# RWKV-5 attention and a SoLU feed-forward block on one core: the decay load on another queue, and a new order for the last chunk

## The chip, the cores and the metric

The kernel runs on one core of a Trainium2 chip. The metric is the device time of one execution in microseconds; lower is better. Besides the plain times there is one profiled execution, with a trace of every instruction and every DMA.

## What is computed

The first half is RWKV-5 attention: for each of 4 batches and 8 heads, a 48 x 48 state is carried over 768 steps and decayed by a vector `w`, with a bonus `u` for the step's own key. The second half is a feed-forward block over the 3072 rows of 384 values that result.

```python
cur = einsum('bhd,bhe->bhde', u * kt, vt)
y[:, :, t] = einsum('bhd,bhde->bhe', rt, state + cur)
state = w[..., None] * state + einsum('bhd,bhe->bhde', kt, vt)
...
h = x @ w_in                               # 384 -> 1024
e = exp(h - max(h)); solu = h * e / sum(e)
ln = (solu - mean) / sqrt(var + 1e-6) * g_ln
out = ln @ w_out                           # 1024 -> 384
```

## The kernel before, in words

The rows are cut into N = 24 chunks of 128 (6 time steps by 4 batches). For each chunk the kernel loads k, r and v, weights them with tables of powers of the decay, forms scores and outputs on TensorE, and then runs the chunk through the feed-forward block. One long function, `direct_path`, writes out the order of all instructions by hand (`manual_schedule`). Every engine works through its own list in exactly the order in which the calls stand, so moving a call moves each instruction that it issues within that engine's list, and each DMA within the list of its queue. Almost every DMA is issued by SyncE (SP). Two small ones are not: `w` by GpSimd (line 493) and `u` by ScalarE (line 496).

**The start.** `w` lands in `wq` (4 x 2 x 48 values). GpSimd issues that DMA as its first instruction of the kernel's own work, then makes the identity matrix `ident`. TensorE runs a few idle multiplications on `ident` (`spin(3)`), turns `wq` into a column (`wd_ps`, line 636), and spreads `u` over the partitions (`u_ps`, line 638). VectorE first clears pads and the score banks (lines 494 to 504). Then it builds the power tables `tab` from `wd_ps` by doubling (lines 643 to 656). From `tab` come the first keys and queries (`turn_r(0)` at 778, `turn_k(0)` at 786), GpSimd's `wide` (line 1313), `weigh(0)` (lines 734 and 735), and everything after them. The first loads of k, r, v and of the weights are all issued ahead of time by SP (lines 594 to 608).

**The feed-forward of a chunk.** `exponential` is on ScalarE. `unit_a` (VectorE, lines 1049 and 1053) makes `solu` and its sum. `unit_b` (ScalarE, line 1061) makes the sum of squares. `deviation` makes from these the factor and shift of the normalisation in four operations on [128 x 1] columns, all on GpSimd: variance (1073), the power -1/2 (1075), the scale (1079) and the shift (1081). `normalise` applies them (ScalarE, 1093). `halve_ln` splits the 32-bit words into 16-bit halves (1118) and starts a DMA transpose on SP (1107). `join_ln` puts the turned halves together again (VectorE, 1112).

**The way out.** Chunks leave in pairs (18 and 19, 20 and 21, 22 and 23 are the last three). `row_sums_12` and `row_sums_34` (VectorE, 1192 to 1198) make sums of halves `s[1]` to `s[4]` of a pair. Seven blocks of 4 matrix multiplications each (line 1202; the trace shows 8 instructions a block) then give both chunks:

- `both_a(l, (0,))` and `(1,)` need only the first chunk of the pair. `(2,)` needs `s[2]`, and so both chunks, and also the copy at 1219 of the bank that it adds to.
- `take_a` adds and copies the banks out (1228, 1230).
- `both_b` has blocks for `s[1]` (its bank is copied out at 1235), `s[3]` and `s[4]`. With `check_sums` a tiny product `n_ps` (706) is put between the last two blocks.
- `both_c` (block for `sums_w[4]`, additions 1249 or 1262 and 1267, a DMA at 1268) and `both_d` (copy at 1278 or 1275, a DMA at 1279 or 1276) finish the pair.

**The checks.** The kernel tests that all weights lie in a range. `check_next` reads one loaded piece with ScalarE (582, `mag`) and has SP load the next piece (524). `check_least` reduces `mag` on VectorE (590). After the 14th piece, `compare_sums` (VectorE, 691 to 700) reduces all tests to one column `low`, which `n_ps` sums on TensorE. If the test fails, a slower general path runs afterwards. Here it doesn't.

The last calls, lines 1771 to 1820, are where the change lies. In them i = 23, j = 21, and l goes through 18, 20, 22.

Of the kernel before, what the change touches and what calls it, by code (L numbers as in the profile page):

```python
# [12 lines left out]
ALU = mybir.AluOpType  # L13
# [386 lines left out]
def direct_path(  # L400
# [29 lines left out]
    nc = tc.nc  # L430
    B, H, S, D = r.shape
# [5 lines left out]
    dff = moe_w_in.shape[1]  # L437
# [47 lines left out]
    wq = const.tile([HP, 2, P], F32, name="wq")  # L485
# [4 lines left out]
    w_out_sb = const.tile([128, KF, dm], F32, name="w_out_sb")  # L490
    decays = const.tile([128, HP], F32, name="decays")

    nc.gpsimd.dma_start(out=wq[:, :, 0:D], in_=w.rearrange("(a q) d -> a q d", q=2))
    nc.vector.memset(wq[:, :, D:], 1.0)
    u_row = u_bc[0:1].rearrange("p h d -> p (h d)")
    nc.scalar.dma_start(out=u_row, in_=u.rearrange("h d -> (h d)").unsqueeze(0))
# [82 lines left out]
    def check_words(j):  # L579
        raw = raws.pop(j)  # L580
        mag = wpool.tile([128, raw.shape[1]], F32, tag="mag", name="mag", bufs=1)
        nc.scalar.activation(out=mag, in_=raw[:, :, 1].bitcast(F32), func=ACT.Abs,
                             accum_out=total[:, j : j + 1])
        mags.append((j, mag))
# [3 lines left out]
    def check_least():  # L588
        for j, mag in mags:
            nc.vector.tensor_reduce(out=least[:, j : j + 1], in_=mag, axis=AX.X, op=ALU.min)  # L590
        mags.clear()
# [32 lines left out]
    neg_half = const.tile([128, 1], F32, name="neg_half")  # L624
# [15 lines left out]
    for vt in vts:  # L640
        nc.scalar.activation(out=vt[:, 1].rearrange("p h x -> p (h x)"),
                             in_=ident[:, 0:1].to_broadcast([128, H * P]), func=ACT.Copy, scale=0.0)
    nc.vector.tensor_scalar(out=pw[:, 0, 0], in0=wd_ps, scalar1=LOW, scalar2=HIGH,
                            op0=ALU.max, op1=ALU.min)
    nc.vector.tensor_copy(out=decays, in_=wd_ps)
    for j in range(8):
# [5 lines left out]
        else:  # L652
            n = 1 << (j - 1)
# [24 lines left out]
    N = len(units)  # L678
    stats = const.tile([128, 5, N], F32, name="stats")
# [388 lines left out]
        unit_a(i)  # L1068
        unit_b(i)

    def deviation(i, j):
        ss, var, rstd = (stats[:, n, i:j] for n in (2, 3, 4))
        nc.gpsimd.tensor_scalar(out=var, in0=ss, scalar1=1.0 / dff, scalar2=1e-6 * dff ** 2,  # L1073
                                op0=ALU.mult, op1=ALU.add)
        nc.gpsimd.tensor_tensor(out=rstd, in0=var, in1=neg_half.to_broadcast([128, j - i]), op=ALU.pow)
        i = max(i, SEVEN)
        if i < j:
            tot, shift, scale, rstd = (stats[:, n, i:j] for n in (1, 2, 3, 4))
            nc.gpsimd.tensor_scalar(out=scale, in0=rstd, scalar1=-float(dff), scalar2=1.0,
                                    op0=ALU.mult, op1=ALU.mult)  # L1080
            nc.gpsimd.tensor_tensor(out=shift, in0=tot, in1=rstd, op=ALU.mult)  # L1081

    def normalise_late(i):
        if SEVEN <= i < N:
# [4 lines left out]
    def normalise(i):  # L1089

        if SEVEN <= i < N:
            solu = live[i]["solu"]
            nc.scalar.activation(out=solu, in_=solu, func=ACT.Identity,  # L1093
                                 scale=stats[:, 3, i : i + 1], bias=stats[:, 2, i : i + 1])
# [16 lines left out]
    def join(words, turned):  # L1111
        nc.vector.tensor_copy(out=words.bitcast(U16).rearrange("p n (t o) -> p o n t", o=2),  # L1112
                              in_=turned)
# [7 lines left out]
    def join_ln(i):  # L1121
        X = live[i]
        if i not in ROOM:
            X["lnT"] = fpool.tile([128, KF, 128], F32, name="lnT")
        else:
            X["lnT"] = bigs[ROOM[i]].rearrange("p (f t) -> p f t", f=KF)
        join(X["lnT"], X["turned"])
# [67 lines left out]
    def row_sums_34(i, engine):  # L1195
        one, two, s = live[i]["lnT"], live[i + 1]["lnT"], live[i]["s"]
        engine.tensor_tensor(out=s[3], in0=one[:, 0:KH], in1=two[:, 0:KH], op=ALU.subtract)
        engine.tensor_tensor(out=s[4], in0=one[:, KH:KF], in1=s[2], op=ALU.subtract)

    def block(dst, rows, weights, start=False):  # L1200
        for f in range(KH):
            nc.tensor.matmul(dst, rows[:, f], weights[:, f], start=(start and f == 0),  # L1202
                             stop=(f == KH - 1), skip_group_check=True)
# [3 lines left out]
    def rows_out(i):  # L1207
        if i < N - 6:
            return fpool.tile([128, dm], F32, name="o")
        return apool.tile([128, H, P], F32, tag="kp", name="kp",  # L1210
                          bufs=5).rearrange("p h d -> p (h d)")[:, 0:dm]

    def both_a(i, which=(0, 1, 2)):
        X = live[i]
        if 0 in which:
            X["o"], X["o2"] = rows_out(i), rows_out(i + 1)
            X["a"], X["e"] = (psM.tile([128, NH], F32, tag="m", name="o_ps") for _ in range(2))
            block(X["a"], X["lnT"][:, 0:KH], upper[:, :, left], True)
            X.get("copy", nc.scalar.copy)(out=X["o"][:, left], in_=X["a"])
        if 1 in which:  # L1220
            block(X["e"], X["lnT"][:, KH:KF], lower[:, :, left], True)
        if 2 in which:
            block(X["a"], X["s"][2], sums_w[2])

    def take_a(i, engine):
        X = live[i]
        if engine == "DVE":
            nc.vector.tensor_tensor(out=X["o"][:, left], in0=X["e"], in1=X["o"][:, left], op=ALU.add)
        else:
            X.get("copy", nc.scalar.copy)(out=X["o"][:, right], in_=X["a"])  # L1230

    def both_b(i, between=None, later=False):
        X = live[i]
        block(X["e"], X["s"][1], sums_w[1], True)
        X.get("copy", nc.scalar.copy)(out=X["o2"][:, right], in_=X["e"])
        if not later:
            both_b2(i, between)

    def both_b2(i, between=None):
        X = live[i]  # L1240
        block(X["a"], X["s"][3], sums_w[3])
        if between:
            between()
        block(X["e"], X["s"][4], lower[:, :, right])

    def both_c_sum(i, also=False):
        X = live[i]
        o2 = X["o2"]
        nc.vector.tensor_tensor(out=o2[:, right], in0=X["a"], in1=o2[:, right], op=ALU.add)
        X["summed"] = True  # L1250
        if also:
            o = X["o"]
            nc.vector.tensor_tensor(out=o[:, right], in0=X["e"], in1=o[:, right], op=ALU.add)
            X["summed"] = 2

    def both_c(i):
        X, Y = live.pop(i), live.pop(i + 1)
        ending[i] = X
        o, o2, a, e = (X[n] for n in ("o", "o2", "a", "e"))
        rows, rows2 = (out[ds(b * S + c * T, T)] for b, c in (units[i], units[i + 1]))  # L1260
        if not X.get("summed"):
            nc.vector.tensor_tensor(out=o2[:, right], in0=a, in1=o2[:, right], op=ALU.add)
        block(a, Y["lnT"][:, KH:KF], sums_w[4])
        if i + 2 == N:
            nc.sync.dma_start(out=rows2[:, right], in_=o2[:, right])
        if X.get("summed") != 2:
            nc.vector.tensor_tensor(out=o[:, right], in0=e, in1=o[:, right], op=ALU.add)
        nc.sync.dma_start(out=rows, in_=o)

    def both_d(i):  # L1270
        X = ending.pop(i)
        (b, c), o2, a = units[i + 1], X["o2"], X["a"]
        rows2 = out[ds(b * S + c * T, T)]
        if i + 2 == N:
            nc.vector.tensor_copy(out=o2[:, left], in_=a)
            nc.sync.dma_start(out=rows2[:, left], in_=o2[:, left])
        else:
            nc.scalar.copy(out=o2[:, left], in_=a)
            nc.sync.dma_start(out=rows2, in_=o2)
# [31 lines left out]
    for q in range(2):  # L1311
        rows = slice(q * P, q * P + D)
        nc.gpsimd.tensor_tensor(out=wide.rearrange("p (a q) -> p a q", q=2)[P : P + D, :, q],
                                in0=back[rows, :, 0], in1=pw[rows, 0, 0], op=ALU.mult)
# [75 lines left out]
    for i in range(LA, LA + LO):  # L1390
        j = i - LA
# [51 lines left out]
    def check_next():  # L1443
        for p in checked:
            check_words(p)
        checked[:] = [checks.pop(0)] if checks else []
        for p in checked:
            load_weights(p, "check", 1)
# [8 lines left out]
    i = LA + LO  # L1457
    j, l = i - LA, 0
    load(i + 5, "kr")
    decay(i + 3)  # L1460
    diagonal(i + 1)
    deviation(0, j)
    ffn_in(j)
    halve_k(i + 3)
# [35 lines left out]
    for i in range(LA + LO + 2, ELEVEN, 2):  # L1500
        j, l = i - LA, i - LA - LO
# [41 lines left out]
        if l == EARLY + 4:  # L1543
            deviation(j, j + 1)
# [86 lines left out]
    for i in range(ELEVEN, N - 1, 2):  # L1631
        j, l = i - LA, i - LA - LO
# [82 lines left out]
    i = N - 1  # L1715
    j, l = i - LA, i - LA - LO
# [62 lines left out]
    both_b(l)  # L1779
    unit_a(i)  # L1780
    unit_b(i)
    deviation(i, N)
    halve_ln(j + 1)
    both_c_sum(l)
    both_c(l)
    join_ln(l + 2)
    join_ln(l + 3)
    row_sums_12(l + 2)
    row_sums_34(l + 2, nc.vector)
    both_d(l)  # L1790
    both_a(l + 2, (0,))
    normalise(i)
    halve_ln(i)
    check_next()

# [2 lines left out]
    both_a(l, (1, 2))  # L1798
    take_a(l, "DVE")
    take_a(l, "ACT")  # L1800
    join_ln(l + 2)
    both_b(l)
    check_least()
    both_c(l)
    both_d(l)
    check_next()
    join_ln(l + 3)
    row_sums_12(l + 2)
    check_least()

    l += 2
    both_a(l)
    take_a(l, "DVE")
    take_a(l, "ACT")
    check_least()
    compare_sums()
    row_sums_34(l, nc.vector)
    both_b(l, check_sums)
    both_c(l)
    both_d(l)  # L1820
# [43 lines left out]
```

## Time and profile before

| what | us |
|---|---|
| runs (median of 3; lowest, highest) | 325.33 (325.25, 325.44) |
| the profiled execution, its own time | 326.05 |
| its span, first to last instruction | 324.3 |
| TensorE busy | 308.9 (95%) |
| VectorE busy | 264.6 (82%) |
| GpSimd busy | 250.9 (77%) |
| ScalarE busy | 245.0 (76%) |
| granted TensorE clock | 0.998 |
| DMA traffic | 52.64 MB, mean 162 GB/s |

How to read it: a busy share is an average over the span, and TensorE's is near its limit. Whether a change of order helps is read in the stage that it touches, from the chain of work that ended last. This chain goes back from the last instruction: at each step it goes to whatever released that instruction, or to the one before it on its engine. By engine, it lies on TensorE for 58% of the span, on GpSimd for 17%, on VectorE for 12%, on waits for a DMA for 3% and on ScalarE for 2%. Timeline rows give start, length, engine, line and operation, and in brackets the idle time of the engine just before the row and what ended it.

### The profile page before, as it was taken

To read this page: it belongs to the slowest core of one execution; us is meant where nothing else is said; L and a number is where in the kernel's file an instruction comes from. 1 tells how busy PE (TensorE), PEld (TensorE's weight loads), DVE (VectorE), ACT (ScalarE), POOL (GpSimd) and SP (SyncE) were. 2 spreads that over 40 slices of the span, in tenths; PEclk is the share of its full clock that TensorE was granted. 3 is DMA by queue.
4 is the path that set the end of the run, shared out by engine and by line. 5 is a ranking of instruction groups with operands and counts; after the bars stand their busy time and mean duration, and the time that the engine had idled before them with its cause. 6 is when DMAs were issued, how large, how long until landed. Compare 5 with 4: busy or idle time off the path is not lost.

```text
span 324.3 us, 9699 instructions
## 1 busy us (share of the span) xinstructions
PE 308.9 (95%) x3903; PEld 216.7 (67%) x3903; DVE 264.6 (82%) x446; ACT 245.0 (76%) x418; POOL 250.9 (77%) x268
## 2 busy tenths in 40 slices
PE   5999999999999999999999999999999999999972
PEld 3875566555456457677678668668677676779972
DVE  6796999998887979999788699789979945868570
ACT  2875888888559788868968969949969978786410
POOL 4899878889999999999999999979978274275000
PEclk9999999999999999999999999999999999999999
DMA  8999999479999998996999999986757535674821
GB/s 165 255 255 200 207 244 169 75 140 139 194 169 173 174 183 144 159 193 106 167 186 164 176 195 225 197 171 133 143 152 161 92 103 147 144 172 102 166 91 61
DMA packets 165800, 52.64 MB, mean 162 GB/s; under 512 B 158321, under 2 KB 161522, under 8 KB 165746
## 3 DMA queue, kind: packets, MB, share of 16 engines
q1 hardware_dynamic: 165712, 51.92, 82.2%
q8 instruction: 33, 0.54, 0.7%
q14 instruction: 21, 0.17, 0.2%
q0 software_dynamic: 32, 0.00, 0.0%
q10 hardware_dynamic: 2, 0.00, 0.0%
HBM read 26.75 MB, written 4.72 MB: 97 GB/s over the span
## 4 chain that ended last, share of the span: by engine, by line
PE 58%; POOL 17%; DVE 12%; issue 5%; DMA 3%; ACT 2%; SPq 0%; POOLq 0%; ACTq 0%; DVEq 0%
PE o_ps L1202 22%; PE h_ps L969 16%; PE h_part L1003 9%; POOL rp L728 3%; POOL rku L734 3%; POOL big L754 3%; POOL kp L721 3%; PE y_ps L881 2%; PE at L819 2%; POOL rku L735 2%; DVE solu L1053 2%; DVE big L832 2%; DMA raw<-in_moe_w_out_dram 1%; PE y_ps L858 1%; PE h_part L881 1%
## 5 line engine op out<-in xcount | busy, mean ns | idle before, releaser
L969 PE MATMUL h_ps<-w_in_sb,xT 128*128 128x512 f32 x216 | 97.0, 598 | 0.0
L969 PEld LDWEIGHTS h_ps<-w_in_sb,xT 128*128 128x128 f32 x216 | 39.9, 190 | 45.1 <-issue 42.4
L1118 ACT COPY halves<-solu 128x2048 uint16<-128x2048 uint16 x23 | 43.6, 1897 | 1.2 <-DVE stats L1049 1.1
L1112 DVE COPY big<-halves 128x2048 uint16<-128x2048 uint16 x21 | 33.7, 1612 | 2.9 <-DMA halves<-halves 2.7
L721 POOL TENSOR_TENSOR kp<-kpad,kdec 128x512 f32<-128x512 f32 x24 | 34.1, 1423 | 0.7
L1112 DVE COPY lnT<-halves 128x2048 uint16<-128x2048 uint16 x18 | 30.1, 1684 | 1.5 <-DMA halves<-halves 1.4
L735 POOL TENSOR_TENSOR rku<-rku,rpad 128x384 f32<-128x384 f32 x24 | 29.0, 1210 | 1.9
L832 DVE COPY_PREDICATED big<-later_half,at 64x512 f32<-64x512 uint32 x40 | 29.4, 736 | 0.7
L734 POOL TENSOR_TENSOR rku<-kpad,u_bc 128x384 f32<-128x384 f32 x24 | 29.8, 1240 | 0.2
L754 POOL TENSOR_SCALAR_AFFINE_SELECT big<-own 64x512 f32<-64x512 f32 x40 | 27.7, 692 | 1.8
L1202 PE MATMUL o_ps<-w_out_sb,ma 128*128 128x192 f32 x160 | 28.1, 328 | 0.0
L1202 PEld LDWEIGHTS o_ps<-w_out_sb,ma 128*128 128x128 f32 x160 | 26.2, 190 | 1.9 <-issue 1.6
L728 POOL TENSOR_TENSOR rp<-rpad,rdec 128x512 f32<-128x512 f32 x15 | 25.5, 1703 | 0.0
L977 ACT ACTIVATE e<-h_ps 128x1024 f32<-128x1024 f32 x18 | 18.4, 1022 | 8.7 <-PE h_ps L969 8.6
L1073 POOL TENSOR_SCALAR stats<-stats 128x1 f32<-128x1 f32 (+2 forms) x14 | 7.2, 516 | 22.7 <-ACT e L1061 22.0
L1061 ACT ACTIVATE e<-solu,stats 128x1024 f32<-128x1024 f32 x20 | 23.0, 1148 | 2.1 <-DVE solu L1053 2.1
L1053 DVE SCALAR_TENSOR_TENSOR solu<-h_ps,stats,e 128x1024 f32<-128x1024 f32 x18 | 23.1, 1284 | 1.5
L1093 ACT ACTIVATE solu<-solu,stats 128x1024 f32<-128x1024 f32 x17 | 21.0, 1232 | 2.4 <-POOL stats L1081 2.4
L1157 PE MATMUL o_ps<-w_out_sb,lnT 128*128 128x384 f32 x64 | 21.6, 491 | 0.0
L1202 PE MATMUL o_ps<-w_out_sb,lnT 128*128 128x192 f32 x112 | 19.8, 330 | 0.0
L956 POOL TENSOR_TENSOR vt<-vt,wide 48x384 f32<-48x384 f32 x16 | 19.1, 1210 | 0.8
L1202 PEld LDWEIGHTS o_ps<-w_out_sb,lnT 128*128 128x128 f32 x112 | 18.3, 190 | 1.6 <-issue 1.4
(196 smaller groups left out, 703.6 us busy)
## 6 DMA issues: line engine op xcount, KB each, us to landing
raw<-in_moe_w_out_dram SPq DMA_DIRECT2D x16, 384.0 KB, 4.1
kpad<-in_k_dram SPq DMA_DIRECT2D x24, 192.0 KB, 5.0
rpad<-in_r_dram SPq DMA_DIRECT2D x24, 192.0 KB, 5.0
vt<-in_v_dram SPq DMA_DIRECT2D x40, 96.0 KB, 3.7
raw<-in_moe_w_in_dram SPq DMA_DIRECT2D x7, 512.0 KB, 6.3
out_dram<-o SPq DMA_DIRECT2D x18, 192.0 KB, 3.1
raw<-in_moe_w_in_dram SPq DMA_DIRECT2D x10, 256.0 KB, 3.4
out_dram<-kp SPq DMA_DIRECT2D x5, 192.0 KB, 3.0
```

The source lines that it names most:

```text
L721: nc.gpsimd.tensor_mul(X["kp"].rearrange("p h d -> p (h d)"), kpads[i % NLD].rearrange("p h d -> p (h d)"), kdec.rearrange("p a d -> p (a ...
L728: nc.gpsimd.tensor_mul(X["rp"].rearrange("p h d -> p (h d)"), rpads[i % NLD].rearrange("p h d -> p (h d)"), rdec.rearrange("p a d -> p (a ...
L734: engine.tensor_mul(rku, kpads[i % NLD][:, :, 0:D], u_bc)
L735: engine.tensor_mul(rku, rku, rpads[i % NLD][:, :, 0:D])
L754: nc.gpsimd.affine_select(out=G[rows, c].rearrange("p a q u -> p (a q) u"), in_=X["own"][rows].to_broadcast([U, H, U]), compare_op=ALU.is_ ...
L832: nc.vector.copy_predicated(X["G"][rows, c].rearrange("p a q u -> p q a u"), later_half[rows].unsqueeze(1).to_broadcast([U, 2, HP, U]), X[ ...
L969: nc.tensor.matmul(h_ps[:, ts(n, NX)], X["xT"][:, j, :], w_in_sb[:, j, ts(n, NX)], start=(j == 0), stop=(j == KD - 1))
L1003: nc.tensor.matmul(dst, rows, weights, start=start, stop=True, skip_group_check=True)
L1053: nc.vector.scalar_tensor_tensor(out=solu, in0=X["h"], scalar=rs, in1=X["e"], op0=ALU.mult, op1=ALU.mult, accum_out=tot)
L1112: nc.vector.tensor_copy(out=words.bitcast(U16).rearrange("p n (t o) -> p o n t", o=2), in_=turned)
L1118: copy(out=both.rearrange("p (o n) -> p o n", o=2), in_=split(X["solu"]))
L1202: nc.tensor.matmul(dst, rows[:, f], weights[:, f], start=(start and f == 0), stop=(f == KH - 1), skip_group_check=True)
```

## The change

Three things are changed.

1. The DMA of `w` is issued by ScalarE instead of GpSimd, ahead of that of `u`.
2. `deviation` is split into `variance`, `root` and `shifts`, which can be put on different engines. For the last chunk (23), `variance` and `shifts` go to VectorE, and only the power stays on GpSimd. They stand between the two joins of the pair 20, 21: the first join, then the variance, the power, `both_c`, the shifts, and the second join. `normalise(23)` now stands before `both_a(20, (0,))` on ScalarE's list; it was behind it. All other calls of `deviation` do as before.
3. In the last two stretches the order of the remaining calls changes. `both_b` of the pair 20 stands before `join_ln(22)`, and one `check_least` is gone. The last `check_next` (which reads piece 13) moves from between `both_d(20)` and `join_ln(23)` to behind the bank copies of `take_a(22)`. `row_sums_34(22)` moves ahead of the last `check_least` and `compare_sums`.

```diff
-    nc.gpsimd.dma_start(out=wq[:, :, 0:D], in_=w.rearrange("(a q) d -> a q d", q=2))
+    nc.scalar.dma_start(out=wq[:, :, 0:D], in_=w.rearrange("(a q) d -> a q d", q=2))
...
+    def variance(i, j, engine):
+        engine.tensor_scalar(out=stats[:, 3, i:j], in0=stats[:, 2, i:j], scalar1=1.0 / dff,
+                             scalar2=1e-6 * dff ** 2, op0=ALU.mult, op1=ALU.add)
+
+    def root(i, j):
+        nc.gpsimd.tensor_tensor(out=stats[:, 4, i:j], in0=stats[:, 3, i:j],
+                                in1=neg_half.to_broadcast([128, j - i]), op=ALU.pow)
+
+    def shifts(i, j, engine):
         i = max(i, SEVEN)
         if i < j:
             tot, shift, scale, rstd = (stats[:, n, i:j] for n in (1, 2, 3, 4))
-            nc.gpsimd.tensor_scalar(out=scale, in0=rstd, scalar1=-float(dff), scalar2=1.0,
-                                    op0=ALU.mult, op1=ALU.mult)
-            nc.gpsimd.tensor_tensor(out=shift, in0=tot, in1=rstd, op=ALU.mult)
+            engine.tensor_scalar(out=scale, in0=rstd, scalar1=-float(dff), scalar2=1.0,
+                                 op0=ALU.mult, op1=ALU.mult)
+            engine.tensor_tensor(out=shift, in0=tot, in1=rstd, op=ALU.mult)
+
+    def deviation(i, j):
+        variance(i, j, nc.gpsimd)
+        root(i, j)
+        shifts(i, j, nc.gpsimd)
...
     both_b(l)
     unit_a(i)
     unit_b(i)
-    deviation(i, N)
     halve_ln(j + 1)
     both_c_sum(l)
+    join_ln(l + 2)
+    variance(i, N, nc.vector)
+    root(i, N)
     both_c(l)
-    join_ln(l + 2)
+    shifts(i, N, nc.vector)
     join_ln(l + 3)
     row_sums_12(l + 2)
     row_sums_34(l + 2, nc.vector)
     both_d(l)
+    normalise(i)
     both_a(l + 2, (0,))
-    normalise(i)
     halve_ln(i)
     check_next()
...
     both_a(l, (1, 2))
     take_a(l, "DVE")
     take_a(l, "ACT")
+    both_b(l)
     join_ln(l + 2)
-    both_b(l)
     check_least()
     both_c(l)
     both_d(l)
-    check_next()
     join_ln(l + 3)
     row_sums_12(l + 2)
-    check_least()
 
     l += 2
     both_a(l)
     take_a(l, "DVE")
     take_a(l, "ACT")
+    check_next()
+    row_sums_34(l, nc.vector)
     check_least()
     compare_sums()
-    row_sums_34(l, nc.vector)
     both_b(l, check_sums)
     both_c(l)
     both_d(l)
```

More of the change, by code (lines that the diff above doesn't have):

```diff
@@ L1069, in unit @@
         unit_b(i)
[L1071 to L1075, printed above, removed]
+    def variance(i, j, engine):
[5 more added lines that the diff above has]
+    def shifts(i, j, engine):
         i = max(i, SEVEN)
```

## The prediction

> **What bounds the kernel now.** I read the page, then the chain of work that ended last, then the timeline where the change lies. At the start the chain is:
>
> ```profile
> 1.45 3.75 DMA wq<-in_w_dram
> ...
> 5.33 0.25 PE wd_ps L636
> ...
> 8.03 0.70 DVE tab L654
> ...
> 9.41 1.01 POOL rku L734
> ```
>
> Columns: start, length, what. Nothing can be decayed before `w` has landed (1.45 + 3.75 = 5.20) and VectorE has built `tab`. The timeline shows what else stood in line:
>
> ```profile
> 0.80 0.51 ACTq L496 DMA_DIRECT2D u_bc<-in_u_dram  x1
> ...
> 1.45 0.81 POOL L493 DMA_DIRECT2D wq<-in_w_dram  x1 [0.95 <-POOLq L1848]
> ...
> 2.56 0.29 POOL masks.py:199 TENSOR_SCALAR_AFFINE_SELECT ident<-ident 128x128 f32<-128x128 f32 x1
> ...
> 3.61 0.06 DVE L634 MEMSET tab<- 128x4 f32 x1
> ...
> 5.60 0.16 DVE L643 TENSOR_SCALAR pw<-wd_ps 128x4 f32<-128x4 f32 x1 [1.93 <-PE wd_ps L636]
> ```
>
> VectorE sat idle 1.93 us for `w`; `ident` too was late, behind GpSimd's DMA. After that no DMA is in the chain until 305.8. From 140 us it is TensorE nearly without a break. At the end:
>
> ```profile
> 296.30 2.27 POOL stats L1073
> 298.65 1.09 POOL stats L1075
> ...
> 300.73 1.25 ACT solu L1093
> 302.01 1.90 ACT halves L1118
> ...
> 305.81 4.49 DMA raw<-in_moe_w_out_dram
> ...
> 311.28 4.17 PE o_ps L1202 x24
> ```
>
> The last chunk's deviation, its normalisation and split, then (behind its transpose on SP's list) the load of the last check, which ScalarE awaits ahead of TensorE's bank copy. Two timeline rows show the contention and the idle time that is to be had:
>
> ```profile
> 296.00 2.53 DVE L1112 COPY big<-halves 128x2048 uint16<-128x2048 uint16 x2
> 296.30 2.26 POOL L1073 TENSOR_SCALAR stats<-stats 128x1 f32<-128x1 f32 x1 [3.53 <-ACT e L1061]
> ...
> 311.28 1.57 PE L1202 MATMUL o_ps<-lows,ma 128*128 128x192 f32 x8 [1.64 <-ACT kp L1219]
> ```
>
> A column of 128 values takes GpSimd 2.26 us: it ends 0.03 after VectorE's two joins do. TensorE's 1.64 us of idle time is all that this tail can give while its work keeps its length.
>
> **What the Trainium skill says.** "SBUF — State Buffer", section "Who interferes with whom": a VectorE copy in a two-port mode holds the port pair that it shares with GpSimd for the whole instruction, and the other blocks; two-input VectorE work in SBUF also contends with GpSimd's reads, work with one input outside those modes doesn't. The trace agrees: line 1073 at least 0.19, here 2.26 beside the joins; line 1075 at 291.66 took 0.56, at 298.65 beside the row sums 1.08. "DMA: Bandwidth & Descriptors", section "Latency and other measured facts": first byte about 0.6 us from ScalarE's or SP's queue, about 1 us from GpSimd's. Here the gap is wider: `w` by GpSimd 3.75 us; `u`, the same 1.5 KB, was issued by ScalarE at 0.80, and ScalarE's wait for its DMA is over by 2.13, the start of its table load: at most 1.33.
>
> **Part 1, w by ScalarE.** `w` now goes at 0.80, where `u` went, and by u's 1.33 lands by about 2.1 instead of 5.2. `u` follows 0.51 later, by about 2.7. GpSimd is rid of the 0.81 us issue and starts `ident` at about 0.85 (VectorE's first row is at 0.86) instead of 2.26, so `ident` is ready near 1.45 instead of 2.85. TensorE's `spin` (2.91, 1.65 long) then ends near 3.15, `wd_ps` (0.25) near 3.45. VectorE clears pads and banks until 3.67 (3.61 + 0.06), so that is late next: `pw` begins at 3.70 instead of 5.60, **1.9 us sooner**. `tab` ends at 6.8. On TensorE `u_ps` (1.61) ends near 5.0, when rpad of chunk 0 lands (1.30 + 3.71 = 5.01), so `turn_r(0)` begins at 5.06 instead of 6.98: also 1.9. `u_bc` on ScalarE (7.09) comes at about 5.0, ahead of `weigh(0)`, now 7.5. If GpSimd doesn't start before 1.45 even without the DMA (its idle time there is charged to its own queue), `ident` is 0.6 later and 1.4 is left: the lower end.
>
> Does it last? The first loads are limited by the DMA engines (90% or more busy in the first slices), not by the compute, and don't come sooner. So I set landing against first use. The tightest of those with a recorded landing is the last w_in piece (issued 13.17, 8.70 to landing, so 21.87; ScalarE's line 537 uses it at 23.50): 1.6 spare, 0.3 short of 1.9. Behind that is ScalarE's diagonal (2.45 long from 24.07, now 22.7 to 25.1), needed by VectorE at 27.28, now 25.4: covered. The rest, rpad of chunk 0 apart, have 2.3 us or more (rpad of chunk 1, landed 9.66, used at 12.44; a w_out piece landed 47.80, used at 50.28); k and r of chunk 8 and later have 10 and more. So 1.9 goes through the chain to TensorE's unbroken stretch and the end. I take 1.9; bounds 1.4 and 1.95.
>
> **Part 2, the deviation.** In times of before: VectorE ends its bank addition (1249) at 295.14. The first join can follow at once (its transpose landed at 290.7): 295.2 to 296.45, half of 2.53. ScalarE's squares with their readout end at 296.22, so the variance runs on VectorE at 296.5 in 0.17 (the [128 x 4] row at 5.60 takes 0.16). The power on GpSimd: 296.7 to 297.3 with 0.56; beside it VectorE has only line 1267 (0.36, one input in PSUM). Bounds 0.56 and 1.08, the row beside row sums. Two shifts on VectorE: 0.25, so at 297.65. ScalarE isn't free: it has `halve_ln(22)` until 298.0 and copy 1278 until 298.22, which hides 0.57 of this chain, all of the upper bound too. So `normalise(23)` runs 298.23 to 299.47, then copy 1219 (0.32), then the split 299.83 to 301.73 instead of 303.91: **2.2 us sooner**. SP has issued its outputs by 301.5; the transpose lands 4.3 later (303.93 to the join at 308.25), at 306.05.
>
> The price is on VectorE: it waits for the power, the second join ends at 298.9 instead of 298.53, and `s[2]` at 300.37 instead of 300.05. TensorE's third block of pair 20 waits for it: 0.3 later than 300.19.
>
> **Part 3, the order at the end.** With `both_b(20)` first, VectorE waits there for the copy at 1235 (303.5 to 303.8), so `join_ln(22)` runs 303.8 to 305.15 instead of 302.32 to 303.65. The check's reduction (0.55) and 1262 (0.36) follow, to 306.06, and the block that overwrites that bank starts at 306.12 instead of 305.58. The two shifts add to 0.54 on TensorE: the first two blocks of pair 22 end for issue at 306.88 + 0.54 + 2.62 = 310.04. The last pair's data: 1267 ends at 306.4, the second join 307.7, `s[2]` 309.2, the copy 1219 at 309.1. So TensorE is late next; the third block begins at 310.04 instead of 311.28: **1.24 us sooner**. Without the delays in the sum it would be 1.64 (upper bound), and with a delay of 1 us instead of 0.54 it would be 0.8.
>
> The last check's load moves behind the transpose on SP's list (about 303.5, lands about 308), its ScalarE work (0.65) falls between copies 1230 and 1235, where ScalarE sat idle 0.98: nothing. On VectorE now the reduction and `compare_sums` come after it: from copy 1230's end (third block + 1.93) 0.68 + 0.5 + 0.82 = 3.93, while `n_ps` stood at + 4.1. Nothing, with 0.15 to spare; without it the delay goes one to one to the end. `row_sums_34(22)` moves ahead: not awaited. I take 1.2 for the tail.
>
> **The sum.** 1.9 + 1.2 = 3.1. Against the profiled execution: 326.05 to 322.95, its span 324.3 to 321.2. That run is 0.72 above the median; against the median, 325.33 - 3.1 = 322.2.
>
> **Rivals.**
> A (as above): own range 321.5 (1.95 + 1.64, and a little scatter) to 323.1 (1.4 + 0.8).
> B: the start lasts, the tail doesn't: VectorE, now holding waits for ScalarE, GpSimd and TensorE in a row, holds back bank adds until TensorE loses the 1.24. For it: TensorE has no gap between 300.19 and 309.5. Against: 0.8 us of spare time for `s[2]`. 325.33 - 1.9 = 323.4, or 323.9 with 1.4.
> C: the start is swallowed on the way, by a load that doesn't come sooner or because GpSimd and VectorE meet differently on their port. Only the tail is left: 324.1. Against: the spare times.
> D: neither lasts, within 0.2%: about 325.2.
> E, slower: the last check. ScalarE's `mag` now stands in TensorE's final sequence, with copy 1235, `compare_sums` and `n_ps` behind it, and TensorE's last blocks behind those. Each microsecond by which its load lands after the point at which ScalarE is free delays the end by one. It has 4.0 us of spare time in my working (308.0 against 312.0), so it decides from a flight of about 8.5 us, and makes the kernel slower than before if part 1 yields nothing and the flight passes about 10.5: 326.3 at 11. Before, it flew 4.49.
>
> **How the numbers follow.** A 0.68, B 0.14, C 0.10, D 0.04, E 0.04. The forecast is A's 322.2. The range must hold A and B (0.82): 321.4 to 323.9. Measurement can tell about 0.2%, 0.65 us, from no change: faster A + B + C = 0.92, same 0.04, slower 0.04.
>
> **What would show it.** Right: `wd_ps` before 3.7 and VectorE's `pw` at about 3.7; rku of chunk 0 near 7.5; the same 1.9 still there in TensorE's rows at 140 us and later; the power at 0.6 on GpSimd, `normalise(23)` straight behind copy 1278; TensorE's idle time before the last pair's third block gone. Wrong: a DMA of k, r or weights in the chain before 60 us, a start shift that shrinks on the way, `n_ps` with a wait for `low`, or bank adds on VectorE that TensorE waits for longer than 0.5.

## The result, and the profile after

Changed kernel: 323.26 us median (22 runs, 322.17 to 327.06). The kernel before, beside it on the same chip: 325.85 (22 runs). Ratio 0.9921, 95% interval 0.9908 to 0.9935: 2.6 us faster (2.1 to 3.0). Forecast were 322.2 and 3.1 us. (The slowest of the 22 fell in a slower state of the chip and is not in the ratio.) The profiled execution of the changed kernel took 323.96 with a span of 322.1; before, 326.05 and 324.3.

The start first: the chain of work that ended last, in the profile of the changed kernel (start, length, what).

```profile
0.79 3.37 DMA wq<-in_w_dram
...
4.29 0.25 PE wd_ps L636
...
8.37 1.01 POOL rku L734
...
20.75 1.01 issue
21.77 0.24 PE y_ps L858
```

`w` leaves 0.66 sooner than before (0.79 against 1.45) but still flies 3.37 us, so `rku` of chunk 0 starts 1.04 sooner (8.37 against 9.41), not 1.9. Then something new stands in the chain: 1.01 us of "issue" at 20.75, in which TensorE waited for nothing that the profile shows. The timeline of the same kernel shows the first microseconds:

```profile
0.79 1.27 ACTq L493 DMA_DIRECT2D wq<-in_w_dram  x1
...
4.29 0.23 PE L636 MATMUL wd_ps<-ident,wq 4*128 4x4 f32 x1 [1.24 <-DMA wq<-in_w_dram]
4.57 0.16 DVE L643 TENSOR_SCALAR pw<-wd_ps 128x4 f32<-128x4 f32 x1 [0.90 <-PE wd_ps L636]
```

The issue of `w` alone took ScalarE's queue 1.27 (u's had taken 0.51). VectorE, done with its clearing, stood 0.90 for `wd_ps`.

The end, from the chain of the changed kernel:

```profile
294.94 1.24 DVE big L1121
296.19 0.04 DVE stats L1072
...
296.30 0.56 POOL stats L1076
...
296.88 0.15 DVE stats L1083
297.03 0.07 DVE stats L1085
297.10 1.26 DVE big L1121
...
299.11 0.70 DVE ma L1202
...
299.95 13.39 PE o_ps L1211 x80
313.34 0.12 PE n_ps L706 x2
```

One join, variance, power, two shifts, second join: the deviation takes 1.0 us (296.08 to 297.10 in the timeline) where GpSimd alone needed 4.4 (296.30 to 300.70). From 299.95 TensorE runs 80 multiplications, ten blocks of 8, without a gap. The load, the split and the 1.64 us ahead of the last pair's third block have left the chain. The TensorE timeline of the changed kernel has that block here, with no idle time ahead of it:

```profile
309.27 1.46 PE L1211 MATMUL o_ps<-lows,ma 128*128 128x192 f32 x8
```

309.27 against 311.28 before: 2.0 sooner. How much of that is the start's? The same TensorE instructions, set against each other in the two traces (after minus before):

| near (us) | 14.7 | 21.8 | 28.5 | 45 | 69 to 213 | from 215.3 | 309 |
|---|---|---|---|---|---|---|---|
| shift (us) | -1.04 | -0.07 | -0.20 | -0.45 | -0.55 | -0.19 | -2.01 |

So in this pair of traces the tail gave 1.8, and the start's 1.04 was cut down at two places, 21.8 and 215.3. Both are rows of TensorE with idle time put down to "issue".

### The profile page after: what moved, and what is told of

Same layout as the page of the kernel before. It is cut to its first block, busy times and chain, and to the rows that moved or that the text cites. A ratio compares the mean times of both kernels' runs of the same rounds, so it can differ in the third digit from the quotient of the medians.

```text
span 322.1 us, 9697 instructions
## 1 busy us (share of the span) xinstructions
PE 307.8 (96%) x3903; PEld 217.0 (67%) x3903; DVE 264.7 (82%) x449; ACT 244.3 (76%) x418; POOL 246.0 (76%) x264
## 4 chain that ended last, share of the span: by engine, by line
PE 63%; POOL 17%; DVE 12%; issue 5%; DMA 1%; ACT 0%; POOLq 0%; DVEq 0%; ACTq 0%
PE o_ps L1211 25%; PE h_ps L969 18%; PE h_part L1003 9%; POOL kp L721 3%; POOL rku L734 3%; POOL rp L728 3%; POOL big L754 3%; PE y_ps L881 3%; PE at L819 2%; POOL rku L735 2%; DVE big L1121 1%; DVE solu L1053 1%; PE h_part L881 1%; DVE big L832 1%; DMA wq<-in_w_dram 1%
## 5 line engine op out<-in xcount | busy, mean ns | idle before, releaser
L1072 POOL TENSOR_SCALAR stats<-stats 128x2 f32<-128x2 f32 (+2 forms) x13 | 4.9, 380 | 19.5 <-ACT e L1061 19.0
L956 POOL TENSOR_TENSOR vt<-vt,wide 48x384 f32<-48x384 f32 x16 | 19.1, 1210 | 0.8
L1211 PEld LDWEIGHTS o_ps<-w_out_sb,lnT 128*128 128x128 f32 x112 | 18.3, 190 | 1.6 <-issue 1.4
```

## The experiments

Ratios are to the kernel before, run beside it, with 95% intervals. A ratio is not the quotient of the two medians beside it and can differ from it by up to 0.002; gains in us are worked out from the ratios. The theories: (1) start and tail add up, as forecast; (2) the start's gain is lost on the way, to a DMA or another engine; later (3), it is lost where TensorE waits for its own instructions.

### One part at a time

`e1_w_only`, on the kernel before:

```
-    nc.gpsimd.dma_start(out=wq[:, :, 0:D], ...
+    nc.scalar.dma_start(out=wq[:, :, 0:D], ...
```

> Only part 1: the DMA of w from ScalarE's queue, the order of the last chunk as before. Theory of the prediction: the start's gain lasts to the end; with the 1.0 us by which w landed sooner in the changed kernel's trace, 1.0 us less than before (ratio 0.997). Rival theory, read from the changed kernel's trace: TensorE reaches the end of a 16 KB page of its instructions at about 20.8 us and stands still until 21.77 for the fetch of the next, which the saturated DMA engines deliver no sooner; the same happens near 215 us. Then only 0.2 to 0.6 us is left at the end (ratio 0.998 to 0.9995), and the trace has TensorE rows without a semaphore's release at 21.8 and 215.3, in both kernels at the same time within 0.2 us.

`e2_tail_only`, on the changed kernel:

```
-    nc.scalar.dma_start(out=wq[:, :, 0:D], ...
+    nc.gpsimd.dma_start(out=wq[:, :, 0:D], ...
```

> Only parts 2 and 3: the new order of the last chunk, w from GpSimd as before. Theory of the prediction: 1.2 us less than before (ratio 0.9963), TensorE's block for s[2] of the last pair late by VectorE's waits. Rival theory, from the changed kernel's trace: TensorE loses its 1.64 us before the last pair's third block and a part of the 0.39 us before the first block of pair 20, so 1.8 to 2.0 us less (ratio 0.9940 to 0.9945).

`e3_deviation_only`: as `e2_tail_only`, with the last two stretches in their old order:

```
-    both_b(l)
     join_ln(l + 2)
+    both_b(l)
     check_least()
     both_c(l)
     both_d(l)
+    check_next()
     join_ln(l + 3)
     row_sums_12(l + 2)
+    check_least()
...
-    check_next()
-    row_sums_34(l, nc.vector)
     check_least()
     compare_sums()
+    row_sums_34(l, nc.vector)
```

> Only part 2: the last chunk's variance and shifts on VectorE between the joins and the earlier normalisation; w and the last two stretches (checks, both_b, row sums) as before. If the deviation is the cause of the tail's gain: 1.5 to 1.9 us less than before (ratio 0.9942 to 0.9955); the last check's load then lands near 308 us and ScalarE's copy after it near 309.0, about when TensorE has done the first two blocks of the last pair. If the move of the check is needed for the gain: below 0.8 us.

`e4_order_only`: as `e2_tail_only`, with the stretch of chunk 23's deviation as before:

```
     unit_b(i)
+    deviation(i, N)
     halve_ln(j + 1)
     both_c_sum(l)
-    join_ln(l + 2)
-    variance(i, N, nc.vector)
-    root(i, N)
     both_c(l)
-    shifts(i, N, nc.vector)
+    join_ln(l + 2)
     join_ln(l + 3)
...
-    normalise(i)
     both_a(l + 2, (0,))
+    normalise(i)
```

> Only part 3: check, both_b and row sums in the new order; w and the last chunk's deviation as before. From the trace of before: s[2] of the last pair ends at 311.03 and the copy behind the check at 311.22, so taking the check away from ahead of the copy is worth 0.2 us at most, 0.0 to 0.2 less than before (ratio 0.9993 to 1.000). Rival: the check's load was the limit by itself and the order alone brings more than 0.8 us.

| | this / before (us) | ratio |
|---|---|---|
| w alone | 325.30 / 325.63 | 0.9982 [0.9971, 0.9994] |
| tail alone | 324.02 / 325.63 | 0.9945 [0.9930, 0.9959] |
| deviation alone | 323.93 / 325.63 | 0.9946 [0.9930, 0.9961] |
| order alone | 325.72 / 325.63 | 0.9997 [0.9984, 1.0011] |

`w` alone is worth 0.6 us, the tail 1.8, together 2.4 of the 2.6 measured. All of the tail is the deviation; the order of the last two stretches is worth nothing that can be measured. With the old deviation TensorE still waits ahead of the last pair's third block: 0.87 us in the trace of the order alone, 1.10 in that of `w` alone, whose timeline has

```profile
296.66 1.05 POOL L1073 TENSOR_SCALAR stats<-stats 128x1 f32<-128x1 f32 x1 [3.52 <-ACT e L1061]
297.79 1.48 POOL L1075 TENSOR_TENSOR stats<-stats,neg_half 128x1 f32<-128x1 f32 x1
...
311.10 1.08 PE L1202 MATMUL o_ps<-lows,ma 128*128 128x192 f32 x5 [1.10 <-ACT kp L1219]
```

So the column of 128 values that took GpSimd 2.26 in the profile of before takes 1.05 here, and the power after it 1.48 instead of 1.08. The 1.64 us of idle time were one run's; four runs with the old deviation (this one, `order alone` and the two with fewer loads below) show 0.87 to 1.11.

### Why only 0.6 of the start?

The trace of `w` alone has the same stop, on TensorE's timeline, behind a row that ended at 20.64. The line under it is the same row in the kernel before:

```profile
21.84 0.30 PE L858 MATMUL y_ps<-big,vt 128*32 128x128 f32 x2 [1.20 <-issue]
```

```profile
21.84 0.30 PE L858 MATMUL y_ps<-big,vt 128*32 128x128 f32 x2 [0.18 <-issue]
```

Before, TensorE came 1.0 later and left at the same time. Counted in the trace, its two stops, at 21.8 and 215, stand ahead of its instructions number 449 and 5825 (from 0), which are 21 times 256 apart, and the trace's packets of the kind "instruction" (the page's DMA queue q8) are 16 KB each. "Runtime: NRT & Kernel Launch" of the Trainium skill, section "Instruction fetch mechanics", says that an engine's instructions are refilled in blocks of 16 KiB, 256 instructions, over a DMA queue of the sequencer's own, and that the cost of crossing a block is mostly hidden. The size agrees with the packets here. "Mostly" agrees too: TensorE has about thirty places 256 instructions apart, and in the trace of the changed kernel it goes through all but two without idle time. At those two the stop is 1.01 and 1.15 us. The packet for the first runs from 19.34 to 20.39 before, 19.28 to 20.27 after and 19.36 to 20.39 with `w` alone (times from the traces' packet records), and TensorE goes on 1.45, 1.50 and 1.45 after its end. In these three the packet's time doesn't depend on when TensorE comes.

All fourteen traces agree: with packets and places taken in order, at none of their 419 places did TensorE go on sooner than 1.29 us after the end of the place's packet, and in all 17 stops of more than 0.1 us it went on between 1.29 and 1.59 after it.

Theory 3 then says: with less traffic on the DMA engines the block comes sooner and w's gain passes. Both of the next kernels load less of w_in ahead of that place. They leave out the last three of its six first pieces and use the first three again in their place; half of w_in is then not the right one, but the work on it is as long:

```
-    load_weights(3)
-    load_weights(4)
-    load_weights(5)
+    for j in (3, 4, 5):
+        spare = wpool.tile([128, NX, 2], U32, tag="raw", name="raw", bufs=6)
+        nc.sync.dma_start(out=spare.rearrange("p n o -> p (n o)")[:, 0:8], in_=pieces[j][1][:, 0:8])
+        raws[j] = raws[j - 3]
```

`e5_fewer_loads_w_gpsimd` is this on the kernel before; `e6_fewer_loads_w_scalar` has `w` by ScalarE as well.

> The kernel before, but of the six first weight pieces the last three (1.5 MB) are not loaded: pieces 0 to 2 are used in their place, so half of w_in is wrong and its work is unchanged. Fetch theory: the DMA engines are done with the backlog sooner, the 16 KB instruction page that TensorE needs at 21.8 us arrives at least 1.5 us sooner than 19.3 + 1.0, and TensorE crosses that page with spare time instead of exactly at its arrival + 1.5; the time changes little by itself, since w is the limit then (0 to 1 us less). Rival, that TensorE's stop at 21.8 is not a fetch through busy DMA engines: the page's arrival and the stop stay where they are.

> The same with fewer loads (pieces 0 to 2 of w_in in place of 3 to 5), and w by ScalarE's queue; the order of the last chunk as before. Fetch theory: against the kernel with fewer loads and w from GpSimd, the whole 1.0 us of w's landing is now there at 28 us and later on TensorE, and about 1.0 us in the time (ratio to the kernel before lower by about 0.003). Rival, that the start's gain is lost for another reason (POOL and VectorE on their port, or late k and r): the two kernels differ by 0.6 us or less, as the two with all loads do.

325.91 and 324.76, both against 326.20: ratios 0.9987 [0.9974, 1.0000] and 0.9952 [0.9933, 0.9971]. Here `w` is worth 1.1 us instead of 0.6; the intervals don't settle that difference. The traces show what happens at the place: the packet begins at 17.62 and 17.03, and TensorE has no stop there in either. The second's timeline (lines are one further down):

```profile
19.95 0.96 PE L859 MATMUL y_ps<-big,vt 128*32 128x128 f32 x26 [0.17 <-DVE big L828]
20.64 0.30 PE L923 MATMUL kv_ps<-vt,kp 128*32 128x48 f32 x6
```

The first of the two passes that place at 21.37, the second at 20.53: 0.84 of lead. It is still 0.85 at 28 us and 0.98 at 211. From 222 on it is 0.7, for the second stops there once more, for 0.30.

Theory 3 can also be tried by moving the place. `e10_fewer_spins`, on the changed kernel, takes 13 of 16 `spin` operations out, which are 26 matmuls and 26 weight loads:

```
-    spin(2)
...
-    spin(4)
...
-    spin(3)
...
-    spin(4)
```

> The changed kernel without 13 of its 16 idle multiplications (52 instructions of TensorE's list, those between 9 and 20 us). Fetch theory: the page's end now lies 52 instructions later in the program, behind the outputs of chunk 1, and TensorE stops there, again until the page's arrival + 1.5 us (about 21.8): the rows of chunk 1's outputs run through about 1 us sooner and the stop shows in the rows that follow; at 28 us 0 to 0.5 us is gained against the changed kernel. Rival, that the stop belongs to those rows (their data or their bank): it stays in the same rows. In the time less than 0.5 us either way[...].

323.36 against 325.47, 0.9918 [0.9887, 0.9949]: within 1 us either way the time is the changed kernel's. What becomes of the first stop this trace can't show: without the idle multiplications the rows from 14 to 19 us ran up to 1.8 times as long (the 32 of line 801 took 1.97 instead of 1.09; why, no run shows), so that TensorE came to its instruction 449 only at 22.76, 2.89 after the packet's end. The second stop, in TensorE's timeline of the changed kernel:

```profile
212.49 1.65 PE L881 MATMUL y_ps<-big,vt 112*32 112x64 f32 x100
...
215.29 0.64 PE L881 MATMUL y_ps<-big,vt 128*32 128x64 f32 x28 [1.15 <-issue]
```

and with fewer spins:

```profile
214.03 1.99 PE L881 MATMUL y_ps<-big,vt 112*32 112x64 f32 x126
...
216.56 0.30 PE L881 MATMUL y_ps<-big,vt 128*32 128x64 f32 x2 [0.55 <-issue]
```

The stop moved from behind the 100th to behind the 126th matmul of the row: 26 matmuls with their 26 weight loads are 52 instructions, the number taken out. In TensorE's instructions it is number 5825 again. The trace shows no releaser at either place. So the stop belongs to a place in TensorE's instruction stream, not to data.

### What sets w's flight?

`e7_u_then_w`, on the changed kernel, issues `u` first:

```
-    nc.scalar.dma_start(out=wq[:, :, 0:D], ...
     nc.vector.memset(wq[:, :, D:], 1.0)
...
     nc.scalar.dma_start(out=u_row, ...
+    nc.scalar.dma_start(out=wq[:, :, 0:D], ...
```

`e8_w_by_sp_first` gives `w` to SP, ahead of its loads of k and r:

```
-    nc.scalar.dma_start(out=wq[:, :, 0:D], ...
+    nc.sync.dma_start(out=wq[:, :, 0:D], ...
```

> The changed kernel with the two DMAs on ScalarE's queue exchanged: u first, then w. What made w take 3.4 us where u had taken at most 1.3? If it is the form of the transfer (eight rows of 192 bytes against one of 1536), u again is through by 2.1 and w, issued at 1.3, lands at about 4.7. If it is the time of issue (the first DMA is ahead of SP's large loads, later ones stand behind them), u is through by 2.1 and w lands later than 4.2 too; the difference is then in w's first packet, which the form theory has right after its issue and the other behind the first packets of kpad. Time within 0.3 us of the changed kernel either way, since the instruction page holds TensorE until 21.8.

> The changed kernel with w issued by SP as the first DMA of all, ahead of kpad of chunk 0. If w waited behind SP's large loads, it now lands at 2.1 to 2.8 us, and VectorE's tables begin at 3.7, when it has cleared its banks; kpad and rpad land about 0.5 us later than before (4.6 and 5.5). If the form of the transfer is slow by itself, w lands at 0.8 + 3.4 = 4.2 again. By the fetch theory the time is within 0.3 us of the changed kernel although the tables start 0.9 us sooner; by the theory of the prediction it is 0.9 us less than the changed kernel (ratio 0.989 to the kernel before).

The start of `u first`, then of `w by SP`, from their timelines:

```profile
1.36 0.76 ACTq L496 DMA_DIRECT2D wq<-in_w_dram  x1
...
5.14 0.23 PE L636 MATMUL wd_ps<-ident,wq 4*128 4x4 f32 x1 [2.08 <-DMA wq<-in_w_dram]
```

```profile
0.79 0.86 SPq L493 DMA_DIRECT2D wq<-in_w_dram  x1
...
2.99 0.26 PE L636 MATMUL wd_ps<-ident,wq 4*128 4x4 f32 x1
3.52 0.15 DVE L643 TENSOR_SCALAR pw<-wd_ps 128x4 f32<-128x4 f32 x1
```

Behind `u`, `w` has a short issue (0.76) and is used only at 5.14; its first packet moves at 3.54 (packet records). By SP, with SP's loads of k and r issued from 1.71 instead of 0.8, it is there by 2.99, without a wait: at most 2.2 us after its issue. "DMA: Bandwidth & Descriptors", section "Issuing engines are not separate DMA queues", says that DMAs run on the same 16 engines and interleave whoever issues them, so that a second issuing engine saves only issuing time. The traces agree: on ScalarE's queue `w` flew 3.4 and 3.6 us beside SP's two loads of 192 KB, 2.2 or less ahead of them. `u` had it short, 1.33, though issued beside the same loads in the kernel before: its packet moved at 1.69, ahead of the first of SP's at 1.91. In the changed kernel SP's begin at 1.90 and w's move from 2.82 to 3.09, among them, which suggests that w's long issue let SP's go first. (The last run changes place and issuing engine together; no run tried ScalarE's queue with SP's loads held back.)

Times: `u first` 323.82 against 326.20, 0.9920 [0.9889, 0.9951]: `pw` is 0.84 later than in the changed kernel. No loss shows, as theory 3 has it, but the interval of 1 us either way could hide one of 0.84. `w by SP`, expected within 0.3 us of the changed kernel, took 322.44, 0.9877 [0.9847, 0.9908]. I repeated it beside the changed kernel (same edit; the other is the changed kernel as it is):

> The changed kernel once more, as it is, on the chip of the next one: ratio about 0.992 by every theory. Its trace shows whether the second stop, near 215 us, is always there: by the fetch theory its length differs from run to run (0 to 1.2 us) with the moment at which the page's 16 KB find their way between the transposes.

> The changed kernel with w as SP's first DMA, again, with more rounds and beside the changed kernel itself. Fetch theory: up to 210 us its rows lie within 0.3 us of the changed kernel's, and the times agree within 0.5 us (the 1.4 us that it seemed to gain lay in the second stop, near 215 us, missed by chance). Rival: w's landing 1.3 us sooner is worth 0.9 us or more.

Changed again: 323.52 against 325.47, 0.9934 [0.9910, 0.9958]. `w` by SP: 321.50, 0.9862 [0.9836, 0.9888]. The intervals don't meet: `w` by SP ahead of the first loads is about 2 us faster than the changed kernel, the fastest version found. This expectation of theory 3 failed: a fetch that holds TensorE to one time whatever came before would have left nothing of it. And 2 us is more than `pw` gains: it begins at 3.52, in the changed kernel's two traces at 4.57 and 4.37. The profiled runs show that the stop does not hold TensorE to one time in every run. In TensorE's timeline of `changed again` there is none at the first place,

```profile
19.87 1.20 PE L858 MATMUL y_ps<-big,vt 128*32 128x128 f32 x26 [0.16 <-DVE big L827]
20.78 0.28 PE L922 MATMUL kv_ps<-vt,kp 128*32 128x48 f32 x4
```

and with `w` by SP one of 0.93 there and, further on, one of 1.02:

```profile
20.71 0.30 PE L858 MATMUL y_ps<-big,vt 128*32 128x128 f32 x2 [0.93 <-issue]
...
214.53 0.64 PE L881 MATMUL y_ps<-big,vt 128*32 128x64 f32 x28 [1.02 <-issue]
```

The packet began at 18.51 and 18.31, and the same kernel's at 19.28 and 18.87 in its other profile. So the stop varies from run to run, by up to 1.5 us. The packet isn't quite fixed either: with all loads kept it began between 19.1 and 19.4 in the five traces in which `w` lands at 5.0 or later, and between 18.3 and 19.4 in the seven in which it lands sooner, so that some of a lead can get through; what moves it, no run here shows. In this pair theory 3 held: `w by SP` was 0.95 ahead at 19.3 us, and 0.05 ahead once its stop was over. The two profiled spans are equal (321.0 and 320.9), for that of `changed again` was its fastest execution and that of `w by SP` its slowest. What the others of `w by SP` gain, no profile here shows; it stays open.

### VectorE or the order?

`e9_deviation_gpsimd`, on the changed kernel, keeps the new order and gives the deviation back to GpSimd:

```
-    variance(i, N, nc.vector)
+    variance(i, N, nc.gpsimd)
     root(i, N)
     both_c(l)
-    shifts(i, N, nc.vector)
+    shifts(i, N, nc.gpsimd)
```

> The changed kernel, but the last chunk's variance and shifts on GpSimd again, in the new order (first join, then the deviation, second join behind it in VectorE's list without a wait). Theory of the prediction: the engine matters, because GpSimd's columns wait for VectorE's second join and row sums (2.26 and 1.08 us in the kernel before): the scale and shift come 1.5 to 2.5 us later than in the changed kernel, of which ScalarE's copies hide about 0.9, and 0.6 to 1.6 us of the gain is lost (ratio to the kernel before 0.994 to 0.997). Rival: the order is what counts; the variance starts in the gap after the first join, the columns get through, and less than 0.3 us is lost (ratio about 0.992 to 0.993).

323.95 against 325.47, 0.9946 [0.9923, 0.9969], beside 0.9934 for the changed kernel: not told apart in time. In the timeline it is:

```profile
295.46 1.33 DVE L1121 COPY big<-halves 128x2048 uint16<-128x2048 uint16 x1
295.50 1.67 POOL L1076 TENSOR_TENSOR stats<-stats,neg_half 128x1 f32<-128x1 f32 x1
...
299.89 1.57 PE L1211 MATMUL o_ps<-lows,ma 128*128 128x192 f32 x8 [1.39 <-ACT kp L1228]
```

The power takes 1.67 beside the join, where it took 0.56 between the joins; it ends 0.38 after the join. That agrees with what the prediction cites from "SBUF — State Buffer" of the Trainium skill, section "Who interferes with whom": the one of the two that comes second is blocked. `normalise` follows at 298.40, and TensorE waits 1.39 at pair 20's third block, for the bank copy behind it on ScalarE, instead of 0.56; ahead of the last pair it has no wait in either. If w's 0.6 is taken off, this order gave 1.2 us without VectorE's help and 1.8 with it (the tail alone); the intervals don't settle how much of that is the engine's.

## Why the prediction was right and where it was wrong

Forecast were 3.1 us, measured 2.6: one term was 1.3 too large and another about 0.6 too small. That the total came out so near is luck: the start stayed below its lower bound of 1.4 and the tail made up half of what was missing. In the prediction's terms the case lay between A and C. Its own signs say so: those for the tail came, those for the start (`wd_ps` before 3.7, rku near 7.5, 1.9 still there at 140 us) didn't, and "a start shift that shrinks on the way" stood among the signs of being wrong. (The medians lie 1.1 apart, since the kernel before ran 0.5 slower beside the changed one than in the times that the forecast started from.)

**Part 1 failed in size: 1.9 forecast, 0.6 measured** (`w` alone, 0.2 to 0.9). Two of its steps:

- "`w` now goes at 0.80, where `u` went, and by u's 1.33 lands by about 2.1". It landed at 4.16. `u` and `w` are the same 1.5 KB but not the same issue (0.51 against 1.27), and w's packets ran among those of SP's loads of k and r. So that VectorE's clearing of pads and banks "is late next" was wrong as well: `pw` began at 4.57, not 3.70. `ident` (needed at 1.41) and `spin` came as forecast. Of 1.9, 1.0 was left.
- "Does it last?" was asked of loads and engines. What TensorE met was its own instructions. The profile of before had the sign: 0.18 and 0.77 us of "issue" on TensorE at 21.8 and 215.5, in rows whose data were ready. I gave them no place in the sum, although a stop that ends at a time of its own leaves no lead to what comes sooner. The 1.0 fell to 0.07 there; about 0.5 grew back by 69 us, in waits that I did not trace.

Rival C ("the start is swallowed on the way") had the effect. At 21.8 its causes were not the ones: no load of k, r or weights stands in the chain there. But the trace of `w` alone has a further loss, at 49 to 50, where TensorE waits 0.76 for VectorE at line 779: from 0.31 ahead of before it falls 0.56 behind. Here the trace points to C's second cause, GpSimd and VectorE meeting differently on their port. From the timelines of `w` alone, then of before:

```profile
41.72 1.28 POOL L721 TENSOR_TENSOR kp<-kpad,kdec 128x512 f32<-128x512 f32 x1
...
41.80 1.41 DVE L571 TENSOR_SCALAR w_out_sb<-ma,minus_g 128x384 f32<-128x384 f32 x1
```

```profile
42.17 0.49 DVE L571 TENSOR_SCALAR w_out_sb<-ma,minus_g 128x384 f32<-128x384 f32 x1
...
42.53 1.28 POOL L721 TENSOR_TENSOR kp<-kpad,kdec 128x512 f32<-128x512 f32 x1
```

With `w` alone GpSimd's product began 0.08 ahead of VectorE's row, which then took 1.41. In the other thirteen traces, none of which has that order, it took 0.42 to 0.55. VectorE carried the 0.9 on to 50 us. How often this happens in the runs without a trace is not known, so the 0.4 us between w's 1.0 at landing and its 0.6 in time are not divided between the stops and this.

**Part 2 was right, and worth more than Part 3 made of it.** The power took 0.56 on GpSimd (forecast 0.56), the variance 0.14 (0.17), `normalise` followed at 297.92 (298.23), the transpose was there for the join at 305.88 (about 306.4).

**Part 3 was forecast at 1.2, with 1.64 as its upper bound; the tail alone measured 1.8 (1.3 to 2.3; the bound lies within).** Two terms. TensorE's delay of 0.54 didn't come: VectorE's first join began at 294.86, not 295.2, everything behind it was sooner, and the block of pair 20 that was to be 0.3 late started at 299.95, 0.24 sooner than before (0.19 of that the start's); the one that was to slip from 305.58 to 306.12 started at 305.33. And the bound forgot a gap that was in the profile, TensorE's 0.39 us at 297.37 for the first join of the two: with the joins pulled apart it went too. From trace to trace: 0.55 there, 1.64 ahead of the third block, 0.18 in rows that ran shorter, less the new wait of 0.56, is 1.81. Against that, the 1.64 belonged to one run (0.87 to 1.11 in four others); from 297.73 to the third block the trace of `w` alone takes 13.37, the changed kernel from the same block 12.65, so with the 0.55 the tail gives 1.3 against that run.

The last check cost nothing, as forecast: `n_ps` ran at 313.27, behind its blocks, and VectorE's `low` was ready at 312.96. Its margin was 0.3 on VectorE. Rival E was further off: its load, issued at 304.07, was not awaited when ScalarE came to it at 310.99, a flight of at most 6.9 where E begins at 8.5. Rival B (VectorE's waits cost the tail) is out: the chain has no wait on VectorE's additions from 299.95 on.

## What to carry to other kernels

Before a gain at the start is counted at the end, look along the bounding engine for idle time put down to "issue" at rows whose data were ready; if it recurs at the same instruction number modulo 256, what is fetched there can come at its own time and take part of a lead. A small load that all else awaits is priced by what lies ahead of it in the shared DMA engines, so put it first in the list that carries the large ones. And a term read from one profile, such as an idle gap of 1.64, wants a second profile before it is taken for the kernel's.

## What the runs showed of the hardware

- TensorE passed most of its crossings of a block of 256 instructions without a stop. At two places, and in one trace at a third, it stopped for up to 1.55 us. It never went on sooner than 1.29 us after the end of the block's 16 KB packet; after a stop, 1.29 to 1.59. At the first place the DMA engines were busy (92% of the first 22 us of the changed kernel).
- 1.5 KB by DMA: 1.3 us to use for `u`, with a short issue; for `w` at most 2.2 ahead of two loads of 192 KB, 3.4 to 3.6 beside them. Its issue takes ScalarE 0.76 or 1.27 us, depending on its place.
- One [128 x 1] operation of GpSimd took 0.19 with VectorE quiet, and 1.05 in some runs, 2.26 in another, beside the same two VectorE copies.
- A VectorE operation on 128 x 384 values took 0.42 to 0.55 in thirteen traces, and 1.41 in the one in which GpSimd had begun a product 0.08 us before it.
